# Attention scores of four heads in one four-bank tile, ordered behind earlier sums, in a fused attention and two-MLP kernel

## Chip, cores and metric

The kernel runs on one core of one Trainium2 chip. The metric is the device time of one execution in microseconds (us); smaller is better. Three runs of the kernel before took 642.29, 642.5 and 643.7 us.

## What is computed

```python
scores = (1/sqrt(64)) * q @ k.T            # 2 batches, 8 heads, 768 positions, 64 per head
keep = (pos < n_sink) | ((rel >= 0) & (rel < window))      # 4 sinks, window 128
a = softmax(where(keep, scores, -1e9))
x = (a @ v), heads side by side            # 1536 tokens x 512
h = x @ w_in                               # first MLP, 512 -> 2048 -> 512
x = (max(h, 0) + alpha * min(h, 0)) @ w_out
h = x @ w_in2                              # second MLP
out = max(h, 0)**2 @ w_out2
```

All of it is float32. The wide matmuls of the MLPs run as three products of a high and a low part (`PR`).

## The kernel before, in words

**Attention** (`Short.job`) is cut into 24 jobs: 12 chunks of 128 tokens (6 of each batch, in the order `ORDER`), each in two groups `g` of four heads. Four of the jobs (the first chunk of either batch) see one block of keys, the other 20 see the block before, the sinks and their own block. A job loads q and K (and v, for the first group), and then on TensorE (PE), VectorE (DVE), ScalarE (ACT) and GpSimd (POOL):

1. scores (PE, L522) of two heads at a time, `p` = 0 and 1, into the tile `s` of two banks; the two heads lie on partitions 0 to 63 and 64 to 127 of q and K. The single-block jobs put `p` = 1 into `ya0` and `ya1`;
2. per `p`: one predicated copy for the diagonal (DVE, L526), then per head a masked reduction that gives the scores and their minimum (DVE, L532, "the reductions" below) and an exponential with its sum (ACT, L536);
3. reciprocal and one scaling of all four heads (DVE, L541 to L548);
4. four transposes into `t` (PE, L556), and one of the sinks' part into `o` (PE, L562); copies of both to SBUF (`pc`, `ss`, on ACT or DVE);
5. two selects (POOL, L570) that part the two key blocks, `pp` and `pc`;
6. the sums a @ v (PE, L588) into `o`, and two copies, a high and a low part, into `X` (L249, L256).

**The MLPs** (`Feed`): the hidden dimension has 16 slices `f` of 128. `half` splits the loaded weights of one slice (input or output half) on DVE and ACT into a high and a low part: on DVE mostly a halving (L291, L293), a combination (L296) and the remainder (L256). `into` (PE, L315) makes h of one slice for a block of tokens in one bank, a unit, and ACT and DVE make `g` from it (L325 to L332). `outof` (PE, L347) adds a slice of g into the bank of output part `j`, and `finish` stores that bank. The first eight slices of the first MLP are done for three blocks of 512 tokens (`EARLY`) while the attention runs; for the first block `into` runs in two parts of 256 tokens, and the output parts `j` run in pairs, in the banks `ya0` and `ya1`. The rest follows when the attention is over (`late`).

**What sets the order.** The engines run fixed lists. `Plan.issue` makes them: each operation has a due time, a cost and what it needs, and the plan gives each engine the operation that can start first, ties by due time; operations with `SOON` go before all others. `JOBS`, `FIRST`, `EARLY_IN`, `EARLY_OUT` and `LOAD` are due times. An engine that waits for one instruction holds up all that stand behind it on its list. `WARM` matmuls of the identity (L696) stand at the start.

PSUM has eight banks: `h0`, `h1`, `ya0`, `ya1`, two of `s`, and one each of `t` and `o`.

Of the kernel before, what the change touches and what calls it, by code (L numbers as in the profile page):

```python
# [18 lines left out]
P = 128  # L19
NS = 32  # L20
# [13 lines left out]

NEAR = 25
# [8 lines left out]
EARLY_OUT = tuple(40 + 2 * f for f in range(8))  # L44
# [7 lines left out]
WARM = 10  # L52


class Plan:
# [4 lines left out]
    def __init__(self, start=()):  # L60
        self.ops, self.written, self.read, self.thin = [], {}, {}, set()
        self.free = dict.fromkeys(AFTER, 0.0)
        self.free.update(start)
# [19 lines left out]
    def until(self, start, cost, ticks, part):  # L83

        while True:
# [3 lines left out]
            ticks[k] = ticks.get(k, 0) + span * rate * part  # L89
# [5 lines left out]
    def issue(self):  # L95
        ops, free, ticks, turns = self.ops, self.free, {}, {}
# [11 lines left out]
        while could:  # L108
# [10 lines left out]
            free[e] = self.until(at, cost, ticks, 0.5 if i in self.thin else 1) if e == "pe" else at + cost  # L119
# [13 lines left out]


class Places:

    def __init__(self):
        self.specs = {}  # L140

    def put(self, pool, shape, dt, *keys):
        for k in keys:
            self.specs[k] = (pool, shape, dt)

    def new(self, key, shape=None, dt=None):
        made = []

        def get():
            if not made:  # L150
                pool, s, d = self.specs[key]
                made.append(pool.tile([P] + (shape or s), dt or d, tag=key, name=key))
            return made[0]
        return get
# [25 lines left out]
def attn_moe_moe(ctx, tc, q, k, v, vsink, par, alpha, w1, w2, out):  # L180
# [80 lines left out]
    class Feed:  # L261
# [3 lines left out]
        def __init__(self, plan, places, raws=lambda q: (q % 3, []), hs=("h0", "h1")):  # L265
            self.plan, self.places, self.raws, self.hs = plan, places, raws, hs
            self.halves = self.banks = 0
            self.w, self.g = {}, {}

        def half(self, due, layer, f, slot, a, need):  # L270
# [5 lines left out]
            r, more = self.raws(q)  # L276
            rk, ck, xk = f"raw{r}", f"cs{q % 2}", f"x{q % 2}"
# [5 lines left out]
            add(due - LOAD + a, more, [rk], ("dma", 1456, lambda: nc.sync.dma_start(out=raw(), in_=src)))  # L283
# [17 lines left out]
        def into(self, due, layer, f, slot, g, chunks, at=0):  # L301
# [3 lines left out]
            hk, rk = self.hs[self.banks % len(self.hs)], f"r{self.banks % 2}"  # L305
            self.banks += 1
# [3 lines left out]
            h, r, gt = new(hk), new(rk), self.g[g]  # L310
            for kt in range(KT):
                def mm(kt=kt):
# [5 lines left out]
                    (["late"] if hk[0] == "y" else []), [hk], ("pe", 3 * (n / 2.4 + 13.3), mm))  # L318
# [18 lines left out]
        def outof(self, due, layer, f, slot, g, j, bank, first, last):  # L337
# [65 lines left out]
    class Short:  # L403
# [3 lines left out]
        def __init__(self, plan, places, con, pool, psum):  # L407
# [7 lines left out]
            put(psum, [2, 512], F32, "s")  # L415
            put(psum, [4, P], F32, "t", "o")

        def add(self, *args):
            self.mine.append(self.plan.add(*args))
            return self.mine[-1]  # L420

        def masks(self):
# [33 lines left out]
            m = self.maskm  # L456
            nc.vector.tensor_scalar_mul(m[:, 0:NS], nosink[:, 0:NS], BIG)
            nc.vector.tensor_scalar_mul(m[:, NS:], outw, BIG)

            inw1 = mrel[:, 0:NS]  # L460
            nc.vector.tensor_scalar(inw1, rel[:, 0:NS], float(P), win_f, op0=ALU.add, op1=ALU.is_lt)
            nc.vector.tensor_tensor(out=inw1, in0=inw1, in1=nosink[:, 0:NS], op=ALU.max)
            nc.vector.tensor_scalar_mul(self.mask1[:, 0:NS], inw1, BIG)
            nc.vector.tensor_copy(out=self.mask1[:, NS:], in_=m[:, NS:])

        def start(self):
            self.K = [self.con.tile([P, 2, 4 * KC], F32, name=f"K{g}") for g in range(NG)]
            self.v, self.early = {}, self.places.new("g7")
# [11 lines left out]
        def job(self, i, b, c, g):  # L480
# [14 lines left out]
            self.load(due - 8, qk, qt, q[b, c, g].rearrange("p (a s) -> p a s", a=2), 364)  # L495
# [348 lines left out]
```

## Time and profile before

| | us |
|---|---|
| three runs: lowest, median, highest | 642.29, 642.5, 643.7 |
| the profiled execution: its own time | 642.0 |
| its span, first to last instruction | 640.3 |
| PE, DVE, ACT, POOL busy in the span | 623.1, 401.3, 240.8, 28.8 |
| first wide matmul (L315) | 29.43 |
| first `outof` matmul (L347) | 80.96 |
| PE's last matmul ends | 633.78 |

The profiled execution took 1.7 us more than its span. Busy time is a sum over instructions; PE's matmuls are pipelined and their ends are modelled, so a PE that is busy all the time can still lose time where it changes from one kind of matmul to another. That is read from the chain of work, where each piece begins where the one before it ends.

### The profile page before, as it was taken

Reading aid. Unit: us, or ns where it says so; the run is one execution under the profiler, and the core shown is the slowest. Engines: PE = TensorE matmul, PEld = TensorE weight load, DVE = VectorE, ACT = ScalarE, POOL = GpSimd, SP = SyncE. Lnnn points to the kernel's source line nnn. Section 1 sums busy time; section 2 is a strip of 40 time slices with the busy share of each in tenths; the row PEclk is TensorE's granted clock in tenths of the full one; section 3 lists DMA queues with packets and bytes.
Section 4 is the critical chain, followed back from the end, with each engine's and each line's share of the span. In section 5 each row is a group of like instructions: output and inputs, shape, how many; then the busy total and the mean of one; then the engine's idle time right before and its main releaser. Section 6 shows DMA issues by size and latency. Waiting matters only on the chain.

```text
span 640.3 us, 9043 instructions
## 1 busy us (share of the span) xinstructions
PE 623.1 (97%) x3400; PEld 511.1 (80%) x3400; DVE 401.3 (63%) x957; ACT 240.8 (38%) x551; POOL 28.8 (5%) x48
## 2 busy tenths in 40 slices
PE   5898999999999999999999999999999999999995
PEld 4697977777888888888888888888888888888884
DVE  7999976677885979445279993333396424344442
ACT  5888844344444725111035671111262211010110
POOL 0011212111200000000000000000000000000000
PEclk9889999999999999999999999999999999999998
DMA  8952322211063445000005540000030000101002
GB/s 277 369 199 71 106 69 66 79 39 34 1 203 127 137 157 167 33 1 0 1 1 167 195 137 29 0 1 0 1 132 1 1 0 1 66 1 42 25 0 72
DMA packets 23429, 48.14 MB, mean 75 GB/s; under 512 B 2512, under 2 KB 11984, under 8 KB 23376
## 3 DMA queue, kind: packets, MB, share of 16 engines
q1 hardware_dynamic: 23232, 47.34, 22.5%
q8 instruction: 29, 0.48, 0.3%
q14 instruction: 24, 0.20, 0.1%
q10 hardware_dynamic: 144, 0.13, 0.1%
HBM read 44.31 MB, written 3.15 MB: 74 GB/s over the span
## 4 chain that ended last, share of the span: by engine, by line
PE 92%; DVE 3%; DMA 3%; SPq 1%; issue 0%; ACT 0%; DVEq 0%; ACTq 0%
PE yb L347 31%; PE h L315 26%; PE ya L315 15%; PE ya L347 11%; PE o L588 4%; PE s L522 4%; PE t L556 1%; DMA Y<-w 1%; DMA K<-k 1%; DMA raw<-w 1%; DVE x L296 0%; DVE x L293 0%; DVE w L256 0%; PE o L562 0%; DVE sp L532 0%; SPq L283 0%
## 5 line engine op out<-in xcount | busy, mean ns | idle before, releaser
L315 PE MATMUL h<-X,w 128*128 128x512 f32 (+1 forms) x816 | 181.5, 371 | 1.1 <-DVE X L249 0.7
L315 PEld LDWEIGHTS h<-X,w 128*128 128x128 f32 x816 | 141.2, 190 | 28.3 <-DVE X L249 0.9
L347 PE MATMUL yb<-w,g 128*128 128x512 f32 x576 | 134.5, 389 | 0.0
L347 PEld LDWEIGHTS yb<-w,g 128*128 128x128 f32 x576 | 108.1, 188 | 22.4
L332 DVE TENSOR_TENSOR r<-r 128x512 f32<-128x512 f32 x48 | 33.1, 691 | 122.8 <-ACT r L330 122.8
L315 PE MATMUL ya<-X,w 128*128 128x512 f32 x432 | 103.9, 389 | 0.0
L315 PEld LDWEIGHTS ya<-X,w 128*128 128x128 f32 x432 | 81.1, 188 | 16.8
L347 PE MATMUL ya<-g,w 128*128 128x512 f32 x288 | 72.8, 400 | 0.0
L256 DVE TENSOR_TENSOR g<-r,g 128x512 fp32r<-128x512 f32 (+1 forms) x104 | 68.6, 659 | 2.5 <-ACT g L249 0.3
L347 PE MATMUL yb<-g,w 128*128 128x512 f32 x288 | 68.3, 390 | 0.0
L347 PEld LDWEIGHTS yb<-g,w 128*128 128x128 f32 x288 | 53.8, 188 | 12.1 <-DVE g L256 1.0
L347 PEld LDWEIGHTS ya<-g,w 128*128 128x128 f32 x288 | 52.1, 188 | 11.6 <-issue 0.2
L287 ACT ACTIVATE cs<-raw 128x512 f32<-128x512 f32 x56 | 37.1, 672 | 39.8 <-DVE x L296 25.5
L330 ACT ACTIVATE r<-ya 128x512 f32<-128x512 f32 x24 | 14.3, 597 | 96.3 <-PE ya L315 96.3
L536 ACT ACTIVATE sp<-sp,nm 128x160 f32<-128x160 f32 (+1 forms) x96 | 40.1, 419 | 26.8 <-DVE nm L532 26.5
L296 DVE SCALAR_TENSOR_TENSOR x<-cs,x 128x512 uint32<-128x512 uint32 x64 | 44.1, 694 | 2.1
L256 DVE TENSOR_TENSOR w<-x,w 128x512 fp32r<-128x512 f32 x64 | 43.9, 688 | 1.2
L330 ACT ACTIVATE r<-h 128x512 f32<-128x512 f32 x24 | 14.4, 598 | 78.2 <-PE h L315 78.2
L327 DVE SCALAR_TENSOR_TENSOR r<-r,oma,h 128x512 f32<-128x512 f32 (+1 forms) x44 | 28.3, 645 | 17.1 <-ACT r L325 16.9
L325 ACT ACTIVATE r<-h 128x512 f32<-128x512 f32 (+1 forms) x44 | 22.8, 517 | 34.1 <-PE h L315 33.8
L522 PE MATMUL s<-K,q 64*128 64x160 f32 (+1 forms) x320 | 32.1, 321 | 1.7 <-issue 1.5
L522 PEld LDWEIGHTS s<-K,q 64*128 64x128 f32 x320 | 24.4, 196 | 11.1 <-issue 8.2
(90 smaller groups left out, 536.8 us busy)
## 6 DMA issues: line engine op xcount, KB each, us to landing
raw<-w SPq DMA_DIRECT2D x56, 512.0 KB, 3.7
Y<-w SPq DMA_DIRECT2D x8, 512.0 KB, 7.0
K<-k SPq DMA_DIRECT2D x24, 160.0 KB, 3.0
v<-v SPq DMA_DIRECT2D x12, 256.0 KB, 2.7
out<-Y SPq DMA_DIRECT2D x11, 256.0 KB, 2.0
q<-q SPq DMA_DIRECT2D x20, 128.0 KB, 2.0
g<-q SPq DMA_DIRECT2D x4, 128.0 KB, 4.6
vs<-vsink SPq DMA_DIRECT2D x2, 256.0 KB, 5.8
```

What stands on the lines that cost most here:

```text
L256: nc.vector.tensor_tensor(out=lo, in0=src, in1=hi.bitcast(F32), op=ALU.subtract)
L287: add(at, [rk], [ck], ("act", 560, lambda: nc.scalar.activation(out=cs(), in_=raw()[:, :, 1].bitcast(F32), func=AF.Abs, scale=2.0 ** -112)))
L296: add(at, [ck, *two(xk)], two(xk), ("dve", dve_ns(512), lambda: nc.vector.scalar_tensor_tensor(out=x(), in0=cs().bitcast(U32), scalar=3, i ...
L315: nc.tensor.matmul(like(h()[:, 0:n], xs), lhsT=wi()[:, a, kt * P:(kt + 1) * P], rhs=xs, start=kt == 0 and i == 0, stop=kt == KT - 1 and i ...
L325: add(SOON + due, [hk], [rk], ("act", act_ns(n, True), lambda: nc.scalar.activation(out=rs(), in_=hs(), func=AF.Relu, scale=-1.0)))
L327: add(SOON + due, [hk, rk, "oma"], [rk], ("dve", dve_ns(n + 60), lambda: nc.vector.scalar_tensor_tensor(out=rs(), in0=rs(), scalar=oma[:, ...
L330: add(SOON + due, [hk], [rk], ("act", act_ns(n, True), lambda: nc.scalar.activation(out=rs(), in_=hs(), func=AF.Relu)))
L332: add(SOON + due, [rk], [rk], ("dve", dve_ns(n), lambda: nc.vector.tensor_tensor(out=rs(), in0=rs(), in1=rs(), op=ALU.mult)))
L347: nc.tensor.matmul(y(), lhsT=lhsT, rhs=rhs, start=first and i == 0, stop=last and i == 2)
L522: nc.tensor.matmul(bank(j)[:, x:y], lhsT=qt()[rows, p], rhs=K[rows, p, k0:k0 + y - x], start=True, stop=True)
L536: ("act", act_ns(n) + 186, lambda h=h: nc.scalar.activation(out=sp()[:, h, 0:n], in_=sp()[:, h, 0:n], func=AF.Exp, scale=-1.0, bias=nm()[: ...
L588: nc.tensor.matmul(po()[j * D:(j + 1) * D, p], lhsT=l, rhs=r, start=x == 0, stop=x == len(terms) - 1)
```

## The change

The scores of a job's four heads become one step, of 16 matmuls in the trace where two steps had 8 each, into one tile `s` of four banks. From the eleventh job on the step is told to follow the sums of the job two places ahead. The banks for that come from `ya0` and `ya1`: during the attention the units (`into`) and the first sums of the MLP (`outof`, now mostly one output part at a time) take turns in `h0` and `h1`. The predicated copy works on four heads. The scaling of step 3 may go to ACT as four instructions. The masks that the first jobs don't need become a planned step, 34 warm-up matmuls stand where 10 stood, due times and load times are new, and the plan counts a switch between kinds of PE work.

```diff
-JOBS = (0, 0.5, 1, 1.5, 12, 16, 20, 24) + tuple(range(40, 120, 5))
+JOBS = (0, 0.5, 1, 1.5, 10, 14, 18, 22) + tuple(range(38, 118, 5))
+JOB_LOADS = (-10, -10, -9, -8.5)
+VALUE_LOADS = {0: -8, 6: -6.5}
+RAW_LOADS = tuple(-9.5 + 1.5 * x for x in range(16))
+NFREE, BEHIND = 10, 2
-WARM = 10
+WARM = 34
...
-            put(psum, [2, 512], F32, "s")
+            put(psum, [4, 512], F32, "s")
...
-            for p in range(2):
-                if c == 0 and p:
-                    sk, both = ["ya0", "ya1"], [new("ya0"), new("ya1")]
-                    bank = lambda j, both=both: both[j]()
-                else:
-                    s, sk = new("s"), ["s"]
-                    bank = lambda j, s=s: s()[:, j]
...
+            s, at = new("s"), due
+            def scores():
+                for p in range(2):
                     for x, y, k0 in ((0, KC, before * KC), (KC, W3, here * KC)) if c else ((0, P, here * KC),):
                         for j in range(2):
                             rows = slice(j * D, (j + 1) * D)
-                            nc.tensor.matmul(bank(j)[:, x:y], lhsT=qt()[rows, p], rhs=K[rows, p, k0:k0 + y - x],
+                            nc.tensor.matmul(s()[:, 2 * p + j, x:y], lhsT=qt()[rows, p], rhs=K[rows, p, k0:k0 + y - x],
                                              start=True, stop=True)
...
+            add(SOON + at, [qk, ("K", g, here)] + ([("K", g, before)] if c else []), ["s"], ("pe", 930 if c else 420, scores),
+                after=self.sums[i - BEHIND] if i >= NFREE else ())
...
-                    add(at, sk, sk, ("dve", dve_ns(2 * P), lambda s=s: nc.vector.copy_predicated(
+                add(at, ["s"], ["s"], ("dve", dve_ns(4 * P), lambda: nc.vector.copy_predicated(
...
+            def each():
+                for h in range(4):
+                    nc.scalar.activation(out=sp()[:, h, win:n], in_=sp()[:, h, win:n], func=AF.Copy, scale=rc()[:, h:h + 1])
             add(due, [rck] + four(spk), four(spk), ("dve", dve_ns(4 * P), lambda: nc.vector.tensor_tensor(
-                out=sp()[:, :, win:n], in0=sp()[:, :, win:n], in1=rc().unsqueeze(2).to_broadcast([P, 4, P]), op=ALU.mult)))
+                out=sp()[:, :, win:n], in0=sp()[:, :, win:n], in1=rc().unsqueeze(2).to_broadcast([P, 4, P]), op=ALU.mult)),
+                ("act", 880, each))
...
-            for js in (range(0, 2), range(2, 4)):
+            for js in ((0, 1), (2,), (3,)) if i == 0 else ((0,), (1,), (2,), (3,)):
+                ys = [feed.bank() for _ in js]
```

How the lists move, at three places.

PE, in the middle of the attention (`ya` and the changed kernel's `h` are banks of output sums, `o<-ss`, `o<-pp`, `o<-pc` the six sums of a job, `s` scores, `t` transposes). Before:

```order
L588 MATMUL o<-pc_1444,v_1190 64x128 x2
L522 MATMUL s<-K_124,q_1401 128x160 x2
L522 MATMUL s<-K_124,q_1401 128x128 x2
L347 MATMUL ya_1194<-g_587,w_1_623 128x512 x3
L556 MATMUL t<-ident,sp_1432 128x128 x4
L562 MATMUL o<-ident,mask_97 128x128
L347 MATMUL ya_1203<-g_587,w_1_623 128x512 x3
L522 MATMUL s<-K_124,q_1401 128x160 x2
```

The first half of a job's scores stood behind sums, the second alone between wide matmuls. Now:

```order
L557 MATMUL t<-ident,sp_1414 128x128 x4
L563 MATMUL o<-ident,mask_94 128x128
L340 MATMUL h_1234<-g_856,w_1_1245 128x512 x3
L340 MATMUL h_1256<-g_856,w_1_1245 128x512 x3
L340 MATMUL h_1498<-g_479,w_1_802 128x512 x3
L340 MATMUL h_1498<-g_509,w_1_890 128x512 x3
L590 MATMUL o<-ss_1481,vs_452 64x128 x2
...
L590 MATMUL o<-pc_1479,v_1162 64x128 x2
L557 MATMUL t<-ident,sp_1468 128x128 x4
L515 MATMUL s<-K_115,q_1424 128x160 x2
L515 MATMUL s<-K_115,q_1424 128x128 x2
L515 MATMUL s<-K_115,q_1424 128x160 x2
L515 MATMUL s<-K_115,q_1424 128x128 x2
```

Both halves stand together behind the sums, here with the transposes of another job between; four groups of wide matmuls part a job's transposes from its sums.

DVE, at the first reductions of the program (`sp,nm<-s,mask`; `x` and `w` are weights being split). Before:

```order
L464 COPY mask_96<-maskm 128x128
L291 TENSOR_SCALAR x_145<-raw_127 128x512
L293 TENSOR_SCALAR x_145<-raw_127 128x512
L296 SCALAR_TENSOR_TENSOR x_145<-cs_143,x_145 128x512
L291 TENSOR_SCALAR x_161<-raw_137 128x512
L249 CAST w_0_164<-x_145 128x512
L293 TENSOR_SCALAR x_161<-raw_137 128x512
L256 TENSOR_TENSOR w_0_164<-x_145,w_0_164 128x512
L296 SCALAR_TENSOR_TENSOR x_161<-cs_159,x_161 128x512
L532 ISA sp_180,nm_181<-s,mask_97 128x128
```

Now:

```order
L462 COPY mask_93<-maskm 128x128
L528 ISA sp_150,nm_151<-s,mask_94 128x128
L528 ISA nm_151 128x1
L528 ISA sp_150,nm_151<-s,mask_94 128x128
L528 ISA nm_151 128x1
L528 ISA sp_150,nm_151<-s,mask_94 128x128
L528 ISA nm_151 128x1
L528 ISA sp_150,nm_151<-s,mask_94 128x128
L528 ISA nm_151 128x1
L284 TENSOR_SCALAR x_165<-raw_137 128x512
```

The first job's reductions moved ahead of the first weight work.

PE, from the last warm-up matmuls (`h<-ident`) to the first wide matmul of the changed kernel:

```order
L699 MATMUL h_330<-ident 128x128
L557 MATMUL t<-ident,sp_253 128x128 x4
L590 MATMUL o<-pc_300,v_211 64x128 x4
L557 MATMUL t<-ident,sp_296 128x128 x4
L590 MATMUL o<-pc_359,v_211 64x128 x4
L515 MATMUL s<-K_114,q_372 128x160 x2
L515 MATMUL s<-K_114,q_372 128x128 x2
L515 MATMUL s<-K_114,q_372 128x160 x2
L515 MATMUL s<-K_114,q_372 128x128 x2
L590 MATMUL o<-pc_382,v_211 64x128 x4
L308 MATMUL h_416<-X,w_0_214 128x256 x6
L308 MATMUL h_429<-X,w_0_290 128x256 x6
```

Four jobs' sums and five jobs' scores stand ahead of it; before, the first half of the sixth job's scores stood there too, and 10 warm-up matmuls instead of 34.

## Rows read from the trace of the kernel before

**Rows 1.** The page: busy time by engine, share of the span, instructions

```profile
PE 623.1 (97%) x3400; PEld 511.1 (80%) x3400; DVE 401.3 (63%) x957; ACT 240.8 (38%) x551; POOL 28.8 (5%) x48
```

**Rows 2.** Busy time by stretch: PE, PEld, DVE, ACT, POOL; granted clock; DMA share, GB/s

```profile
0.00:10.00 10.00, 5.93 (x30) 5.37 (x30) 7.25 (x31) 3.35 (x5) 1.14 (x8) 1.00 0.77 243
10.00:20.00 10.00, 7.13 (x42) 5.15 (x44) 8.79 (x44) 8.98 (x34) 0.00 (x0) 1.00 0.99 363
20.00:29.00 9.00, 7.21 (x54) 5.43 (x56) 9.00 (x33) 8.25 (x27) 0.00 (x0) 0.99 1.05 371
29.00:36.00 7.00, 6.89 (x41) 5.45 (x39) 6.97 (x24) 5.45 (x14) 1.41 (x2) 0.53 0.96 350
36.00:81.00 45.00, 43.22 (x432) 38.53 (x429) 44.81 (x146) 37.09 (x108) 7.68 (x10) 1.00 0.35 106
81.00:179.00 98.00, 98.00 (x812) 75.72 (x811) 68.20 (x235) 43.44 (x148) 18.62 (x28) 1.00 0.16 45
179.00:640.00 461.00, 454.74 (x2004) 375.44 (x2002) 256.31 (x455) 134.28 (x223) 0.00 (x0) 1.00 0.18 59
```

**Rows 3.** The chain of work in the middle of the attention: start us, us, what

```profile
99.68 1.46 PE o L588 x24
101.14 0.69 PE s L522 x8
101.83 0.90 PE ya L347 x3
102.73 0.44 PE t L556 x4
103.17 0.11 PE o L562
103.28 0.70 PE ya L347 x3
```

**Rows 4.** The chain of work, its first piece of L347

```profile
80.96 0.70 PE ya L347 x3
```

**Rows 5.** DVE's timeline at the last unit of the first block: start us, us

```profile
80.61 0.42 DVE L526 COPY_PREDICATED s<-tri,s 128x256 f32<-128x256 uint32 x1
80.94 0.68 DVE L548 TENSOR_TENSOR sp<-sp,rc 128x512 f32<-128x512 f32 x1
81.55 0.47 DVE L327 SCALAR_TENSOR_TENSOR r<-r,oma,h 128x256 f32<-128x256 f32 x1
```

**Rows 6.** Groups of DVE's instructions, 0 to 180 us: busy us, mean ns

```profile
L296 DVE SCALAR_TENSOR_TENSOR x<-cs,x 128x512 uint32<-128x512 uint32 x18 | 12.7, 712 | 0.1
L256 DVE TENSOR_TENSOR w<-x,w 128x512 fp32r<-128x512 f32 x16 | 11.0, 688 | 0.0
...
L293 DVE TENSOR_SCALAR x<-raw 128x512 uint16<-128x512 uint16 x10 | 4.3, 446 | 0.0
```

**Rows 7.** PE's timeline at the start

```profile
2.72 4.63 PE L696 MATMUL h<-ident 128*128 128x128 f32 x20 [2.72 <-POOL ident L439]
...
7.91 0.80 PE L522 MATMUL s<-K,g 64*128 64x128 f32 x4 [0.55 <-DMA K<-k]
...
29.43 1.01 PE L315 MATMUL h<-X,w 128*128 128x256 f32 x3
```

**Rows 8.** PE's waits in 0 to 70 us: total, times, longest

```profile
PE s L522 <- DVE nm L532: 2.0, 4, 0.8
```

**Rows 9.** The timeline of one job from its transposes to its sums

```profile
102.57 0.60 PE L556 MATMUL t<-ident,sp 128*128 128x128 f32 x4
...
103.27 0.69 DVE L249 COPY pc<-t 128x512 f32<-128x512 f32 x1 [0.31 <-PE o L562]
...
103.67 0.42 ACT L536 ACTIVATE sp<-sp,nm 128x160 f32<-128x160 f32 x1
...
104.73 0.64 POOL L570 TENSOR_SCALAR_AFFINE_SELECT pc<-pc 128x512 f32<-128x512 f32 x1
...
106.20 0.44 PE L588 MATMUL o<-ss,vs 128*64 128x128 f32 x4
```

More of the change, by code (lines that the diff above doesn't have):

```diff
@@ L51 @@
 NEND = 4
-WARM = 10
+WARM = 34
 class Plan:
     def __init__(self, start=()):
-        self.ops, self.written, self.read, self.thin = [], {}, {}, set()
+        self.ops, self.written, self.read, self.kind = [], {}, {}, {}
         self.free = dict.fromkeys(AFTER, 0.0)
@@ L81, in add, with until @@
         return i
-    def until(self, start, cost, ticks, part):
+    def until(self, start, cost, ticks):
         while True:
@@ L88, in until @@
             span = min((k + 1) * TICK - start, cost / rate)
-            ticks[k] = ticks.get(k, 0) + span * rate * part
+            ticks[k] = ticks.get(k, 0) + span * rate
             cost -= span * rate
@@ L95, in issue @@
     def issue(self):
[L96 removed]
+        ops, free, ticks, turns, kind = self.ops, self.free, {}, {}, None
         then, left, ready = [[] for _ in ops], [len(o[1]) for o in ops], [[0.0] * len(o[2]) for o in ops]
@@ L118, in issue @@
             _, cost, run = ops[i][2][x]
-            free[e] = self.until(at, cost, ticks, 0.5 if i in self.thin else 1) if e == "pe" else at + cost
+            if e == "pe":
+                kind, last = self.kind.get(i), kind
+                free[e] = self.until(at, cost + (SWITCH if kind != last else 0), ticks)
+            else:
+                free[e] = at + cost
             if ops[i][3]:
@@ L276, in half @@
             r, more = self.raws(q)
+            early = RAW_LOADS[q:q + 1] if self.early else ()
             rk, ck, xk = f"raw{r}", f"cs{q % 2}", f"x{q % 2}"
@@ L282, in half @@
             at = due - PARTS + a
-            add(due - LOAD + a, more, [rk], ("dma", 1456, lambda: nc.sync.dma_start(out=raw(), in_=src)))
+            add(early[0] if early else due - LOAD + a, more, [rk], ("dma", 1456, lambda: nc.sync.dma_start(out=raw(), in_=src)))
             half = lambda dt, j: x().bitcast(dt).rearrange("p (j w) -> p j w", w=2)[:, :, j]
@@ new lines, in job @@
+            self.plan.kind[self.mine[-1]] = "scores"
+            if c:
+                add(at, ["s"], ["s"], ("dve", dve_ns(4 * P), lambda: nc.vector.copy_predicated(
+                    out=s()[:, :, W3 - P:W3], mask=self.tri.unsqueeze(1).to_broadcast([P, 4, P]), data=s()[:, :, 0:P])))
+            for h in range(4):
+                at = due + .4 * h
+                add(at, ["s", "masks" if c else "mask0"], [(spk, h), (nmk, h)], ("dve", dve_ns(n) + 8, lambda h=h:
+                    nc.vector.tensor_tensor_reduce(
+                        out=sp()[:, h, 0:n], in0=s()[:, h, lo:lo + n], in1=mask, scale=-SCALE, scalar=3e38,
+                        op0=ALU.add, op1=ALU.min, accum_out=nm()[:, h:h + 1])))
+                add(at + 1, [(spk, h), (nmk, h)], [(spk, h), (smk, h)],
+                    ("act", act_ns(n) + 190, lambda h=h: nc.scalar.activation(
+                        out=sp()[:, h, 0:n], in_=sp()[:, h, 0:n], func=AF.Exp, scale=-1.0,
+                        bias=nm()[:, h:h + 1], accum_out=sm()[:, h:h + 1])))
@@ L588, in mm @@
                             nc.tensor.matmul(po()[j * D:(j + 1) * D, p], lhsT=l, rhs=r, start=x == 0, stop=x == len(terms) - 1)
-                add(SOON + due + 2, [x for _, need in terms for x in need], ["o"], ("pe", 205 * len(terms) + 100, mm))
+                self.sums[i].append(add(SOON + due + 2, [x for _, need in terms for x in need], ["o"],
+                                        ("pe", 205 * len(terms), mm)))
+                self.plan.kind[self.sums[i][-1]] = "sums"
             xs = [X[:, e, 2 * g:2 * g + 2, ci * P:(ci + 1) * P] for e in range(2)]
```

107 lines of the change are left out of this document (43 added, 64 removed).

## The prediction

> **What bounds the kernel now.** I read the busy times first: PE is busy 623.1 of 640.3 us [rows 1]. By stretch [rows 2] the reader should see three regimes. From 81 us to the end PE never stops (98.00 of 98.00, then 454.74 of 461 with the last stores behind it), so there only fewer or cheaper PE steps gain anything. From 20 to 81 us DVE is full (9.00 of 9, 6.97 of 7, 44.81 of 45) and PE is full too but for 0.11 us and 1.78 us; whichever gets more work loses. Before 20 us neither is full: DVE idles 2.75 + 1.21 = 3.96 us, PE 6.9 us. From 29 to 36 us the granted clock is 0.53, that is, nearly all at 1.2 of 2.4 GHz, after PE had idled 1.79 of the 9 us before. Busy PE hides what a step really takes, so prices come from the chain of work [rows 3].
>
> I cut the program at the first matmul of L347, 80.96 us [rows 4], which needs nearly the same work done in both kernels, and price the two sides apart.
>
> **Behind the cut: PE's price.**
>
> *Merged scores.* A step of scores takes 0.69 us in the chain, and the three wide matmuls behind it 0.90 instead of 0.70, 0.20 more [rows 3]. So a step alone among wide matmuls costs 0.89 us. Put behind the other half it saves the way in and out. Its eight matmuls then cost between 0.69 (no gain inside the step) and little more than the streams; the nearest row is the sums, 24 small matmuls without a change of kind in 1.46 us, 0.061 each, 0.49 for eight. I take 0.49: saving 0.40 a job, bounds 0.20 (only the 0.20 behind it) and 0.45. By the lists twelve jobs' scores stand behind the cut: 12 × 0.40 = **4.8** (2.4 to 5.4).
>
> *A page against it.* In the trace the eight weight loads of a step fit, with all else, in 0.69 us. The Trainium skill ("TensorE: Matmul & The Clock Gate", "LDWEIGHTS" and Part 3) gives columns/1.2, so 107 ns for 128 columns, and says that a load overlaps running matmuls only where its row group differs; one after another eight loads would be 0.85 us, the merge would save 0.04 a job, and the sum would lose 12 × 0.36 = 4.3 us, an estimate from that page. The trace speaks against that reading: 0.69 is less than 0.85, so the two row groups' loads run beside each other.
>
> *What is owed at the cut.* By the lists, before still owes 25 half steps of scores, 14 sets of transposes and 14 of the sinks' transposes there; the changed kernel owes 24, 13 and 13; the sums are 14 in both. That is 0.89 + 0.44 + 0.11 = **1.4** less [rows 3]; its other side is in the front.
>
> *Transposes between sums and scores.* Four times behind the cut the list has sums, transposes, scores: one change of kind more each. Bounds 0 and 0.20 (what wide matmuls paid behind scores); I take 0.20, as it lies nearest: **−0.8**.
>
> *New stalls.* The last operations before a job's sums run in series: transposes at 102.57, a copy, two selects that end at 104.73 + 0.64 = 105.37, sums at 106.20 [rows 9]: 2.80 needed, 0.83 spare. In the changed list the same stretch holds the transposes, the sinks' transposes and four groups of wide matmuls, 0.44 + 0.11 + 4 × 0.70 = 3.35 [rows 3]: 0.55 spare. And the copy stands on ACT in 20 of 24 jobs (16 before), where an exponential takes 0.42 [rows 9]. A copy one exponential late just fits, two are 0.29 late. Bounds 0 and 0.29 × 14 = 4.1; I take 0.05 a job, as most copies should find the queue that the plan expects: **−0.7**.
>
> *Single output parts in `h0`, `h1`.* A part's bank is wanted again two groups later, 24 wide matmuls or 8 × 0.70 = 5.6 us on; the copy to SBUF is hidden under that. In the first block parts 0 and 1 end together and part 2 waits for part 0's copy as it did in `ya0`: nothing. If the cover went, each would cost about one copy, 0.69 us [rows 9], three to five times.
>
> **Ahead of the cut: DVE's price.** DVE's last operation that belongs ahead of the cut is the reading of the first block's last unit, at 81.55 us [rows 5]. Counted in the lists up to it, the changed kernel has 5 scalings fewer at 0.61 each (80.94 to 81.55 [rows 5]; they go to ACT as four instructions each), 15 predicated copies of 256 at 0.33 (80.61 to 80.94) against 8 of 512 at up to twice that (I take 0.60), one weight combination and one remainder fewer and three halvings fewer (0.71, 0.69 and 0.45 [rows 6], each less the 0.07 to 0.10 by which neighbours overlap: 0.62, 0.60, 0.36), but 3 copies of the transposes more (0.69 [rows 9], so 0.60): 3.05 + 0.15 + 1.22 + 1.08 − 1.80 = 3.7 us less DVE work. ACT has the room: 37.09 of 45 us, and the scalings that moved are three in the first 40 us.
>
> DVE's idle 3.96 us can shrink, since q and K are loaded ahead of the first weights (before, the first scores waited for K until 7.91 us) [rows 7] and the reductions come first; it can also grow, because the weight splitting that filled those gaps now stands behind them. Its bounds: 3.96 gained, or, with the low clock below, some 5.7 lost. I take 1 us lost, near no change, since both reasons hold. So the front is **+2.7**, bounds −2 and +7.6.
>
> What PE would allow there is more: clock 0.47 × 7 = 3.3 us, idle 1.9, eight merged steps 3.2, and an earlier first wide matmul. DVE's list ahead of the last remainder of the fourth job's X is shorter by two combinations, three remainders, three scalings and a few reductions less three copies, over 4 us, so the first wide matmul should come at about 25 instead of 29.43 [rows 7]. PE will then wait for split weights: what it gains there beyond DVE's 2.7 is lost again in waits.
>
> *Warm-up.* 10 instructions (20 matmuls) took 4.63 us [rows 7], so 24 more are up to 11 us at 1.2 GHz, half at 2.4. PE idles 4.07 + 2.87 + 1.79 = 8.7 us in the first 29 [rows 2]. At the higher clock they hide; if the clock stays low they delay the first jobs by 11 − 8.7 = 2.3 us and more where idle time falls in the wrong place: that is the low end of the front.
>
> *Loads.* K of the fifth job stands behind eight weight loads and all early q, K and v on SP's queue, one of those loads waiting for DVE and ACT to free its buffer: 6.0 MB at 363 GB/s [rows 2] is 17 us, about 19 us with the start, before its scores are due: nothing. If it slipped, scores and all of PE's list would wait.
>
> **Sum.** 4.8 + 1.4 − 0.8 − 0.7 + 2.7 = 7.4 us. The profiled execution took 642.0 (span 640.3 and 1.7 around it): 634.6. The median of the runs, 642.5, is 0.5 above it; from there it is 635.1, and I predict **635.0 us**.
>
> **Rivals.**
>
> *A. The one tile stalls every job (slower).* With two half steps, scores of `p` = 1 waited for the reductions of `p` = 0. Now the scores of a job need all four reductions of the job before, and behind the waiting scores stand all wide matmuls. For it: while DVE is full its list runs late, and PE waited four times for that, 2.0 us, 0.8 the longest [rows 8]. Against it: the job before had its scores one set of sums earlier, 106.20 − 99.68 = 6.5 us [rows 3, 9], and DVE has 30 of 98 us free behind the cut. At 0.8 us in each of 20 jobs, 16 us: 635 + 16 = 651. It decides once the waits pass 7.4 / 20 = 0.37 us a job. Chance 0.08.
>
> *B. The front opens.* DVE's idle goes instead of growing, the clock rises early and stays. The front gives 7.6 instead of 2.7: 630. The clock row speaks for it: the clock fell after idle time that 24 more matmuls fill. The Trainium skill ("TensorE: Matmul & The Clock Gate", "HAM oscillation") says likewise that waits between bursts of matmuls let the clock fall back. Against it is DVE's full list. Chance 0.22.
>
> *C. The front loses.* Warm-up matmuls at the low clock and new gaps on DVE: −2 instead of +2.7, 639.7. Chance 0.15.
>
> *D. The merge saves only the change behind it,* because the second half costs a full 0.69: 0.20 a job, 2.4 instead of 4.8: 637.4. What the Trainium skill's page on TensorE says of loads, above, leans this way. Chance 0.08.
>
> *E. Transposes to sums too tight:* 4.1 instead of 0.7: 638.4. Chance 0.07.
>
> **How the numbers follow.** My forecast, 632 to 638, has 0.40. The range 628 to 641 holds it with B, C, D and E but for their tails, and leaves out A. A change under 0.2%, 1.3 us, can't be told from none here. Slower: A and a tenth of C and E together, 0.09. Same: 0.04. Faster: 0.87.
>
> **What would show it.** In the chain behind the cut: scores as one piece of 16 of about 1.2 us behind sums (0.69 + 0.49; more than 1.35 means D), PE without idle time, the first L340 matmul at 77 to 79 us. At 74 B holds, at 82 C. Waits of scores for the reductions of more than 7 us in total mean A; waits of sums for POOL of over 3 us mean E. The first wide matmul should come at about 25 us with the clock at 1.00 behind it. I am wrong if the gain lies mostly ahead of the cut, or if PE is idle for some us between the cut and the attention's end.

## The result, and the profile after

The changed kernel took 633.98 us, median of four runs (632.97 to 635.78); the kernel before, on the same chip, 642.61 (642.29 to 643.7). The ratio is 0.9866, 95% interval 0.984 to 0.9892: 8.6 us faster. The forecast was 635.0, range 628 to 641, so the time, its sign and the likeliest case held. Not all of the steps did.

The profiled execution of the changed kernel is the slowest of its four: 635.78 us, span 634.1. Against the profiled one of before (642.0, 640.3) the gain is 6.2 us, and this is the number to hold against the sum of 7.4. Of the other three the time and the mean granted clock are on record: 634.45 us at 0.996, 633.5 and 632.97 at 0.999; the profiled one has 0.994.

Busy time on the page, to be read against [rows 1]:

```profile
PE 618.5 (98%) x3448; PEld 512.4 (81%) x3448; DVE 390.3 (62%) x927; ACT 248.5 (39%) x579; POOL 29.1 (5%) x48
```

Busy time by stretch, columns as in [rows 2]; the cut at 81 us is the same, behind it the attention now ends near 172 us:

```profile
0.00:10.00 10.00, 7.28 (x41) 6.56 (x42) 5.42 (x31) 3.96 (x12) 1.14 (x8) 1.00 0.71 199
10.00:20.00 10.00, 9.51 (x79) 8.29 (x80) 8.58 (x38) 7.74 (x31) 0.00 (x0) 1.00 0.98 357
20.00:29.00 9.00, 7.59 (x52) 5.85 (x51) 7.39 (x20) 6.53 (x17) 0.00 (x0) 0.62 0.91 312
29.00:36.00 7.00, 6.72 (x62) 6.26 (x61) 7.00 (x25) 6.74 (x22) 0.00 (x0) 1.00 0.80 264
36.00:81.00 45.00, 40.90 (x427) 36.42 (x425) 45.00 (x147) 40.70 (x121) 10.38 (x13) 1.00 0.48 144
81.00:172.00 91.00, 90.44 (x791) 72.84 (x790) 66.55 (x235) 47.94 (x160) 17.59 (x28) 1.00 0.21 61
```

From 81 us to the end of the attention PE still hardly stops. Ahead of it DVE is full from 29 to 81 us and PE no longer is: 4.1 us idle from 36 to 81 where it had 1.78. In the first 29 us DVE works 5.42 + 8.58 + 7.39 = 21.39 us; before it was 7.25 + 8.79 + 9.00 = 25.04 [rows 2]. So its idle time there grew by 3.65 us.

The chain of work in the middle of the attention, in order of time (start, us, what), against [rows 3]:

```profile
105.22 0.59 PE t L557 x4
105.80 1.19 PE s L515 x16
106.99 0.26 PE o L563
107.25 1.40 PE h L340 x6
...
110.11 1.19 PE s L515 x16
111.30 0.90 PE h L340 x3
112.20 0.44 PE t L557 x4
```

The scores of four heads are one piece of 1.19 us between sums and wide matmuls. The three wide matmuls behind it still pay the way out, 0.90 us. A job's scores used to cost 2 × (0.69 + 0.20) = 1.78; they now cost 1.19 + 0.20 = 1.39.

PE's timeline at its first wide matmul and at its first matmul of L340 (L347 before), the cut, against [rows 4, 7]:

```profile
27.80 2.43 PE L308 MATMUL h<-X,w 128*128 128x256 f32 x14
...
79.76 0.71 PE L340 MATMUL h<-g,w 128*128 128x512 f32 x2
```

PE's waits from 78 to 180 us, all that there are:

```profile
PE o L563 <- DVE mask L542: 0.4, 1, 0.4
```

From the cut to the start of PE's last matmul it was 552.6 us (80.80 to 633.38) and is 548.1 (79.76 to 627.86). So 4.5 us came from behind the cut, where 4.7 were forecast, and 1.0 from ahead of it, where 2.7 were. The other 0.7 lie behind the start of PE's last matmul, where none were: the span ended 6.9 us after it and now ends 6.2 after it, as in every other run below (6.15 to 6.35). (The cut of before is 80.96 in the chain and 80.80 in the record of the matmul itself; I use the record from here on.)

Busy time from the start to the cut, first before, then now:

```profile
0.00:80.80 80.80, 70.18 (x586) 59.74 (x587) 76.62 (x268) 63.06 (x181) 10.22 (x20) 0.96 0.61 205
0.00:79.76 79.76, 70.75 (x648) 62.36 (x648) 72.16 (x253) 64.42 (x195) 11.26 (x20) 0.96 0.64 204
```

DVE has 4.46 us less work there (72.16 against 76.62) and 3.42 us more idle time (7.60 against 4.18). The difference is the 1.0 us.

### The profile page after: what moved, and what is told of

Read it like the earlier page. It is cut to its first block, busy times and chain, and to the rows that moved or that the text cites. A ratio compares the mean times of both kernels' runs of the same rounds, so it can differ in the third digit from the quotient of the medians.

```text
span 634.1 us, 9086 instructions
## 1 busy us (share of the span) xinstructions
PE 618.5 (98%) x3448; PEld 512.4 (81%) x3448; DVE 390.3 (62%) x927; ACT 248.5 (39%) x579; POOL 29.1 (5%) x48
## 4 chain that ended last, share of the span: by engine, by line
PE 80%; DVE 13%; DMA 3%; issue 1%; SPq 1%; ACT 1%; DVEq 0%; ACTq 0%
PE h L308 35%; PE yb L340 28%; PE h L340 10%; PE o L590 4%; PE s L515 3%; DVE w L247 2%; DVE x L289 2%; DMA al<-alpha 2%; DVE r L320 1%; DVE x L286 1%; PE t L557 1%; DVE g L247 1%; DVE sp L528 1%; DMA raw<-w 1%; DVE X L247 1%
## 5 line engine op out<-in xcount | busy, mean ns | idle before, releaser
L308 PE MATMUL h<-X,w 128*128 128x512 f32 (+1 forms) x1248 | 275.9, 375 | 0.3 <-DVE r L320 0.3
L308 PEld LDWEIGHTS h<-X,w 128*128 128x128 f32 x1248 | 222.3, 189 | 42.8 <-DVE r L320 0.7
L340 PE MATMUL yb<-w,g 128*128 128x512 f32 x576 | 134.5, 389 | 0.0
L340 PEld LDWEIGHTS yb<-w,g 128*128 128x128 f32 x576 | 108.1, 188 | 22.4
L323 ACT ACTIVATE r<-h 128x512 f32<-128x512 f32 x48 | 28.7, 598 | 174.5 <-PE h L308 174.4
L340 PE MATMUL h<-g,w 128*128 128x512 f32 x288 | 69.5, 395 | 0.1
L340 PE MATMUL yb<-g,w 128*128 128x512 f32 x288 | 68.7, 391 | 0.2 <-DVE g L247 0.2
L340 PEld LDWEIGHTS yb<-g,w 128*128 128x128 f32 x288 | 53.7, 188 | 12.7 <-DVE g L247 1.6
L340 PEld LDWEIGHTS h<-g,w 128*128 128x128 f32 x288 | 53.2, 189 | 11.4 <-ACT Y L240 0.6
L320 DVE SCALAR_TENSOR_TENSOR r<-r,oma,h 128x512 f32<-128x512 f32 (+1 forms) x56 | 37.2, 666 | 36.3 <-ACT r L318 36.3
L240 DVE CAST g<-r 128x512 fp32r<-128x512 f32 (+1 forms) x69 | 29.1, 422 | 2.8
L240 DVE CAST w<-x 128x512 fp32r<-128x512 f32 x25 | 10.6, 425 | 28.8 <-PE h L308 18.6
L240 ACT CAST w<-x 128x512 fp32r<-128x512 f32 x39 | 24.0, 616 | 7.1 <-DVE x L289 6.4
L286 DVE TENSOR_SCALAR x<-raw 128x512 uint16<-128x512 uint16 x56 | 25.5, 460 | 1.0 <-DMA raw<-w 0.8
```

The source lines that it names most:

```text
L240: return lambda: f(**dict(zip(("out", "in_"), get())))
L286: add(at, [rk], [(xk, 0)], ("dve", dve_ns(512, True), lambda: nc.vector.tensor_scalar(half(U16, 0), raw().bitcast(U16).rearrange("p j (w a ...
L308: nc.tensor.matmul(like(h()[:, 0:n], xs), lhsT=wi()[:, a, kt * P:(kt + 1) * P], rhs=xs, start=kt == 0 and i == 0, stop=kt == KT - 1 and i ...
L320: add(SOON + due, [hk, rk, "oma"], [rk], ("dve", dve_ns(n + 60), lambda: nc.vector.scalar_tensor_tensor(out=rs(), in0=rs(), scalar=oma[:, ...
L340: nc.tensor.matmul(y(), lhsT=lhsT, rhs=rhs, start=first and i == 0, stop=last and i == 2)
```

## Experiments

Each edit is to the changed kernel unless it says otherwise. "Behind the cut" is the time from the first matmul of L340 to the start of PE's last one, in the profiled execution. The kernel before took 641.7 to 642.1 us beside these runs.

| run | median us | ratio to before, 95% interval | cut us | behind the cut us |
|---|---|---|---|---|
| before | 642.61 | 1 | 80.80 | 552.6 |
| changed kernel | 633.98 | 0.9866 (0.984 to 0.9892) | 79.76 | 548.1 |
| a2_again | 633.83 | 0.9871 (0.9855 to 0.9886) | 80.01 | 547.5 |
| x1_foreign | 642.26 | 1.0013 (1.0002 to 1.0023) | 79.36 | 554.9 |
| x2_same | 637.18 | 0.9925 (0.9912 to 0.9938) | 79.00 | 551.0 |
| x3_nobehind | 635.2 | 0.9899 (0.9884 to 0.9913) | 78.33 | 548.5 |
| x4_warm10 | 636.97 | 0.9923 (0.9903 to 0.9942) | 81.06 | 547.4 |
| x5_front | 652.01 | 1.0145 (1.0129 to 1.0162) | 94.43 | 551.6 |
| x6_noact | 634.58 | 0.9885 (0.987 to 0.99) | 78.28 | 548.2 |
| x7_warm60 | 636.68 | 0.9923 (0.9909 to 0.9936) | 80.94 | 547.4 |
| x8_dve | 645.19 | 1.0044 (1.003 to 1.0058) | 88.77 | 548.1 |
| x9_pool | 642.76 | 1.0008 (0.9999 to 1.0017) | 94.02 | 540.7 |
| x10_oldtimes | 633.16 | 0.9867 (0.9851 to 0.9882) | 74.18 | 551.0 |
| x12_old34 | 633.02 | 0.9862 (0.9846 to 0.9879) | 73.69 | 551.4 |

The last two columns can be compared where the lists owe the same attention at the cut. Against the changed kernel x9 owes two jobs' scores and sums fewer, x10 and x12 one job more, x3, x6 and x7 one job's transposes more (0.55 us by the chain), and the kernel before half a step of scores and one job's transposes more (the 1.4 us of the forecast).

**The merge: part the two halves again.** x1 puts one identity matmul between the halves of each of the 20 two-block jobs, x2 two more score matmuls of the same kind; the second half of the scores writes over both.

```diff
 for p in range(2):
+    if c and p:      # x1
+        nc.tensor.matmul(s()[:, 3, 0:P], lhsT=self.ident, rhs=self.ident, start=True, stop=True)
...
+    if c and p:      # x2
+        for j in range(2):
+            rows = slice(j * D, (j + 1) * D)
+            nc.tensor.matmul(s()[:, 2 + j, 0:P], lhsT=qt()[rows, p],
+                             rhs=K[rows, p, here * KC:here * KC + P], start=True, stop=True)
```

> The changed kernel with one identity matmul of another kind (128 rows instead of 64, 128 columns) put between the two halves of the scores of each of the 20 two-block jobs; its result is overwritten, the lists are otherwise the same. Theory 1 (the gain behind the first outof is the way in and out of a kind of matmul that the merge saves, about 0.4 us a job): each of the 20 costs one way out and in plus its own two passes, some 0.3 to 0.4 us; the 12 behind the first outof count in full, those ahead are partly hidden by DVE: 4 to 7 us more than the changed kernel's 634.0, so 638 to 641, and more than the variant with two more matmuls of the same kind. The piece of scores in the chain grows from 1.19 us to 1.5 or more. Rival (the gain comes from less DVE work and the new loads, a change of kind costs no more than its stream): 20 times 0.11 at most, about 1.5 us, 635.5, and less than the same-kind variant.

> The changed kernel with two more matmuls of 128 columns of the same kind (64 rows, both row halves) between the two halves of each two-block job's scores; their result is overwritten. Both theories: only their streams, four passes in two pairs, 0.1 to 0.25 us a job, 12 behind the first outof in full: 1.5 to 3.5 us more than 634.0, so 635.5 to 637.5. Theory 1 says that this is less than the variant with one foreign matmul, the rival that it is more.

The chain of work of x1, in the same place:

```profile
106.04 0.59 PE t L559 x4
106.62 0.69 PE s L517 x8
107.32 0.42 PE s L512 x2
107.73 0.69 PE s L517 x8
```

And that of x2:

```profile
104.64 0.59 PE t L562 x4
105.22 0.69 PE s L520 x8
105.92 0.22 PE s L514 x4
106.14 0.49 PE s L520 x8
```

In x2 the second half is a piece of its own, 0.49 us: the estimate that was taken from the sums' 0.061 a matmul. In x1, behind a foreign matmul, it is 0.69 again, and the foreign matmul takes 0.42 where the two of the same kind take 0.22. x1 holds less work than x2 and is 5.1 us slower. So it is the change of kind that costs. Twelve jobs behind the cut at 0.20 + 0.42 = 0.62 are 7.4 us; behind the cut x1 lost 554.9 − 548.1 = 6.8. One needless matmul a job takes away all that the change gives. The eight jobs ahead of the cut pay the same price, 5.0 us in all, and the cut did not come later (79.36 against 79.76). But 79.76 is from the changed kernel's slowest execution. By the medians x1 lost 8.3 us, 1.5 more than behind the cut: PE has room ahead of it for most of the 5.0 us, not for all.

**The place behind the sums.** x3 takes away the rule that the scores follow the sums of the job two places ahead; the merged tile stays.

```diff
-NFREE, BEHIND = 10, 2
+NFREE, BEHIND = 99, 2
```

> The changed kernel without the rule that puts scores behind the sums of the job two places ahead (each job's scores are still one step of four heads). Changes of kind on PE's list from the first wide matmul on: 73 instead of 66 (94 in the kernel before). Theory 1 (0.2 us for each change): 7 more, 1.4 us, about 635.4. Rival (placement is what counts, merging the halves is not): most of the gain behind the first outof goes, 4 us or more, 638 or more.

It took 635.2 us, about 1.2 more than the changed kernel, which is just what can't be told from nothing here. Behind the cut it is 548.5 against 548.1, with 0.55 us more owed. PE's list has 73 changes of kind from the first wide matmul on (transposes counted with the wide matmuls), against 66 with the rule and 94 in the kernel before. The seven lie behind the cut, and the 0.2 us that was expected for each does not show there. The tile merges the halves; the rule adds little.

**DVE sets the front.** x8 doubles the early weights' remainders (the second result is the same as the first and written over it), which adds 16 operations of some 0.6 us to DVE.

```diff
+low = lo_op(lambda: (w()[:, 1], x().bitcast(F32), w()[:, 0]), 512)
+if early:
+    low = (("dve", low[0][1], lambda go=low[0][2]: (go(), go())),)
-add(at + 2, [*two(xk), (wk, 0)], [(wk, 1)], *lo_op(lambda: (w()[:, 1], x().bitcast(F32), w()[:, 0]), 512))
+add(at + 2, [*two(xk), (wk, 0)], [(wk, 1)], *low)
```

> The changed kernel with each of the 16 early weight remainders done twice on DVE (0.6 us each, 9.6 us in all, the same result; the plan does not know of it, so all lists are otherwise the same). Theory 1 (DVE bounds the front): the first outof comes 6 to 10 us later than at 79 us and the total rises by as much, 640 to 644. Rival (chains of waits or PE bound it): 3 us or less, 637 or less.

The cut came at 88.77 instead of 79.76, 9.0 us later for 9.6 us of work, and behind it nothing changed (548.1); by the medians it lost 11.2. With x1 this is the pair that was wanted: of 5.0 us more work on PE ahead of the cut some 1.5 reach the time, of 9.6 on DVE nearly all or all.

**Can work be taken from DVE?** x6 lets no scaling go to ACT; x9 lets the early remainders go to GpSimd (`low` is that of x8, undoubled; 14 of 16 went).

```diff
-    in1=rc().unsqueeze(2).to_broadcast([P, 4, P]), op=ALU.mult)),
-    ("act", 880, each))
+    in1=rc().unsqueeze(2).to_broadcast([P, 4, P]), op=ALU.mult)))      # x6
...
+if early:                                                              # x9
+    low += (("pool", 1200, lambda: nc.gpsimd.tensor_tensor(
+        out=w()[:, 1], in0=x().bitcast(F32), in1=w()[:, 0].bitcast(F32), op=ALU.subtract)),)
```

> The changed kernel with all 24 scalings on DVE, as before (the changed kernel has 6 on ACT, 5 of them ahead of the first outof). Changes of kind 68 instead of 66. Theory 1 (DVE's full list bounds the front): 5 times 0.61 = 3 us more DVE work ahead of the first outof, 1.5 to 4 us more than 634.0. Rival (ACT's chains bound it as much, or PE): within 1 us of 634.0.

> The changed kernel with the plan free to put the 16 early weight remainders on GpSimd (14 of them go there: 8.4 us of DVE work less ahead of the first outof). Theory 1: DVE is eased, the front gains until PE or the chains bind, 2 to 5 us less than 634.0, 629 to 632, if GpSimd takes not much more than the 1.2 us that the plan assumes. Rival (chains bind, or GpSimd's longer operations delay the selects and the splitting): 634 or more.

Both missed. x6 took 634.58 us, and its cut, 78.28, is not later. Its stretch from 36 to 81 us:

```profile
36.00:81.00 45.00, 42.92 (x433) 37.88 (x432) 45.00 (x142) 35.07 (x102) 9.25 (x12) 1.00 0.42 128
```

DVE is full there as in the changed kernel, and ACT has 35.07 us of work instead of 40.70. Up to its cut DVE has 10 scalings instead of 6, some 2.5 us more, but two halvings and two casts to `g` fewer, and its busy time there is 72.70 us against 72.16. The plan puts other operations that have a choice in the place of the scalings, so which engine a scaling goes to decides little.

x9 took 642.76 us, no better than the kernel before. Groups of its first 90 us, by shape (busy us, mean ns, idle time before):

```profile
L294 POOL TENSOR_TENSOR w<-x,w 128x512 fp32r<-128x512 f32 x14 | 18.8, 1350 | 36.2 <-ACT w L240 34.7 <-DVE w L240 1.4
L289 DVE SCALAR_TENSOR_TENSOR x<-cs,x 128x512 uint32<-128x512 uint32 x18 | 14.0, 787 | 0.0
L247 DVE TENSOR_TENSOR g<-r,g 128x256 fp32r<-128x256 f32 x14 | 8.8, 630 | 0.0
```

The same two groups on DVE in the changed kernel, and the remainders that are on DVE there:

```profile
L289 DVE SCALAR_TENSOR_TENSOR x<-cs,x 128x512 uint32<-128x512 uint32 x18 | 12.5, 696 | 0.0
L247 DVE TENSOR_TENSOR w<-x,w 128x512 fp32r<-128x512 f32 x16 | 10.9, 682 | 0.0
L247 DVE TENSOR_TENSOR g<-r,g 128x256 fp32r<-128x256 f32 x16 | 7.3, 459 | 0.0
```

GpSimd needs 1350 ns for what DVE does in 682, and some of DVE's own operations stretch: 459 to 630 ns and 696 to 787 in the mean. They are few: of the 14 subtractions for `g` four took 847 to 1499 ns, the other ten 406 to 418, and three of the four ran while GpSimd subtracted. So a remainder that is worth 0.6 us on DVE gives part of that back. The plan also filled DVE's list again: up to the cut it has 12 casts to `g` instead of 6 and 7 copies of the sinks' part instead of 1, and ACT 4 and 1 instead of 9 and 6; two jobs' scores and sums more stand ahead of the cut here, which explains part of these counts. PE's waits ahead of the cut are for DVE's scalings (5.3 us), `X` (3.5) and masks (1.5), none of them for weights from GpSimd. How much of the 8.8 us each of these takes wasn't parted.

**The new times alone, and the change without them.** x5 is the kernel before with the new due times, load times and 34 warm-up matmuls; x10 is the changed kernel with all times and the 10 warm-up matmuls of before. The edit of x10:

```diff
-JOBS = (0, 0.5, 1, 1.5, 10, 14, 18, 22) + tuple(range(38, 118, 5))
+JOBS = (0, 0.5, 1, 1.5, 12, 16, 20, 24) + tuple(range(40, 120, 5))
-EARLY_OUT = tuple(44 + 2 * f for f in range(8))
+EARLY_OUT = tuple(40 + 2 * f for f in range(8))
-WARM = 34
+WARM = 10
...
-when = JOB_LOADS[i] if i < 4 else due - 8
+when = due - 8
```

> The kernel before with the changed kernel's due times, load times and 34 warm-up matmuls, but with scores in half steps, the banks ya0 and ya1, the copy per half and all scalings on DVE as before. Changes of kind on PE's list from the first wide matmul on: 100 (94 before, 66 in the changed kernel). Theory 1 (behind the first outof only the merge gains, ahead of it only what DVE is spared): the clock is up early, but DVE's list is as long as before: 0 to 2 us less than before from the earlier start, 1 us more for 6 changes, so 640 to 643. Rival (the loads and the warm-up open the front by themselves): 3 us or more less than before, 639 or less.

> The changed kernel with all times of the kernel before (jobs' due times, first sums' due times, load times, 10 warm-up matmuls); the scores' one tile, the banks, the plan's switches and the place behind the sums stay. Theory: behind the cut nothing changes, 547.5 to 549.5 us from the first L340 matmul to PE's last; the front loses what early loads and warm-up give (scores wait for K until 7.9 us again, and the run with 10 warm-up matmuls lost 3 us): first L340 at 80.5 to 84, total 636.5 to 640. Rival (the new times give nothing, as the run with the times alone was slower than the kernel before): within 1 us of the changed kernel or faster, first L340 at 79 or earlier. If the front's new times and the merge only work together, the total is above 641.

> The changed kernel once more, unaltered, so that its neighbours in this batch have it on their own chip. Theory: 633 to 635 us, 7 to 9 below the kernel before. Its profile shows which of the two sides of the cut (the first matmul of L340 that sums the MLP) varies between executions: I expect 548 to 548.5 us from the cut to PE's last matmul again, and all variation, up to 1.5 us, ahead of it (78.3 to 80).

x5 missed both expectations: 652.01 us, 10 slower than the kernel before. Its cut came at 94.43; its stretch from 36 to 81 us:

```profile
36.00:81.00 45.00, 38.22 (x322) 32.23 (x322) 43.13 (x133) 34.85 (x97) 7.42 (x10) 0.85 0.44 141
```

PE is idle for 6.8 us there and DVE for 1.9, at a clock of 0.85. Why the old banks and the new times fit so badly was not taken further. But x5's lists owe the same at the cut as the changed kernel's (24 half steps of scores, 13 sets of transposes, 14 of sums), so the two can be compared behind it: 551.6 against 548.1 and 547.5. That is 3.5 to 4.1 us for the merge, with its transposes and stalls, where the steps made 4.8 − 0.8 − 0.7 = 3.3.

x10 missed the theory too, and here the rival held: 633.16 us, against 633.83 for the changed kernel on the same chip. **The new times give nothing; all of the gain is in the tile, the banks and the plan that goes with them.** The first 29 us of x10 in one stretch, and then the changed kernel's:

```profile
0.00:29.00 29.00, 17.28 (x124) 13.38 (x124) 24.43 (x100) 21.14 (x68) 1.14 (x8) 0.82 0.87 291
```

```profile
0.00:29.00 29.00, 24.37 (x169) 20.70 (x170) 21.40 (x88) 18.23 (x58) 1.14 (x8) 0.88 0.87 288
```

DVE, which sets the front, does 24.43 us of work there with the old times and 21.40 with the new. DVE's waits in the same 29 us say why; of the changed kernel, and then of x10:

```profile
DVE sp L528 <- PE s L515: 1.3, 2, 1.1
DVE parf L443 <- DMA pari<-par: 1.3, 1, 1.3
DVE pp L437 <- POOL pc L430: 1.2, 1, 1.2
DVE x L286 <- DMA raw<-w: 0.8, 1, 0.8
DVE rc L537 <- ACT sp L532: 0.7, 1, 0.7
DVE x L284 <- DMA raw<-w: 0.6, 1, 0.6
DVE oma L695 <- DMA al<-alpha: 0.5, 1, 0.5
DVE s L522 <- PE s L515: 0.4, 1, 0.4
DVE X L240 <- PE o L590: 0.4, 1, 0.4
```

```profile
DVE parf L443 <- DMA pari<-par: 1.3, 1, 1.3
DVE pp L437 <- POOL pc L430: 1.2, 1, 1.2
DVE rc L537 <- ACT sp L532: 0.6, 2, 0.3
DVE x L284 <- DMA raw<-w: 0.5, 1, 0.5
DVE sp L528 <- PE s L515: 0.3, 1, 0.3
DVE x L284 <- DMA Y<-w: 0.3, 1, 0.3
```

The rows add up to 7.2 and 4.2 us, so they hold the whole difference of 3.0. DVE waits for PE 2.1 us instead of 0.3 (scores, the first sums) and for loads, `par` aside, 1.9 instead of 0.8: the reductions stand ahead of the splitting that used to fill such gaps, and q and K are loaded ahead of the weights. PE's scores start earlier, 5.58 instead of 7.98 us, and PE is not what the front waits for. Part of the 3.0 us belongs to the one execution: x3 runs the changed kernel's lists on PE, DVE, ACT and GpSimd until 60 us, and there DVE works 22.82 us in the first 29. At the cut x10 owes one job more than the changed kernel: scores 1.39, two sets of transposes 0.88, the sinks' 0.11 and sums 1.46, together 3.8 by the chain; 551.0 is 2.9 more than 548.1 and 3.5 more than 547.5.

The changed kernel once more (a2) took 633.83 us with 547.5 behind the cut, 0.5 less than the lower end expected. Again the profiled execution, 635.61, was the slowest of its four.

**Warm-up and clock.** The changed kernel with 10 and with 60 warm-up matmuls, and x10 with 34:

```diff
-WARM = 34
+WARM = 10      # x4_warm10; 60 in x7_warm60
```

> The changed kernel with 10 warm-up matmuls as before instead of 34. Theory 1 (the front is bound by DVE's list and the chains of the first jobs; the warm-up raises the clock in the first 22 us, and shortens those chains): 0.5 to 2 us more than 634.0. Rival (PE's clock in the front decides): 3 us or more, 637 or more, with the granted clock at half until about 29 us or later. If the warm-up only fills idle time: no change.

> 60 warm-up matmuls instead of 34. Theory (DVE's list sets the front; the clock costs something only where PE has no room left): the clock stays high until the first wide matmul, first L340 matmul at 78 to 79 us, total within 1 us of the changed kernel on the same chip. Rival 1 (the low clock still costs the changed kernel its front): 1.5 us or more faster, first L340 at 77 or earlier. Rival 2 (warm-up matmuls stand in the way of the first jobs' scores and sums): 1.5 us or more slower, first L340 at 80.5 or later.

> The kernel with the times of before (x10_oldtimes), now with 34 warm-up matmuls instead of 10. There the granted clock was 0.55 from 10 to 20 us while PE was busy 5.75 of 10 us. Theory (PE has room in the front, DVE's list sets it): the clock is 1.00 from 10 us on, and the total stays within 1 us of x10_oldtimes, 632.5 to 634.5. Rival 1 (the low clock costs the front): 630 to 632. Rival 2 (warm-up matmuls delay the first jobs, as 60 did with the new times): 635 or more. If it comes out at 636 to 637 like 10 and 60 with the new times, the number of warm-up matmuls acts by the order the plan makes of it, not by the clock.

With the new times both edits lose: 636.97 is 3.0 us above 633.98, and 636.68 is 2.9 above 633.83, on the same chip. With the old times 10 and 34 are the same, 633.16 and 633.02. Stretches of the start, of x7, x10 and x12 in this order (the column before the last two is the granted clock):

```profile
10.00:20.00 10.00, 10.00 (x85) 8.93 (x84) 9.38 (x44) 8.74 (x34) 0.00 (x0) 1.00 0.99 374
```

```profile
10.00:20.00 10.00, 5.75 (x36) 4.12 (x36) 8.27 (x38) 8.87 (x35) 0.00 (x0) 0.55 0.98 347
```

```profile
10.00:20.00 10.00, 9.01 (x80) 7.63 (x80) 8.52 (x48) 8.90 (x36) 0.00 (x0) 1.00 1.00 361
```

x10 runs this stretch at 0.55 and x12 at 1.00, for the same time. x7 runs at 1.00 all through and is slow: PE is busy 10.00 of 10 and then 9.00 of 9, and the first wide matmul comes at 30.28 instead of 27.80, behind the warm-up. So with the old times the clock of the first 30 us decides nothing.

With the new times it does count. The 36 matmuls from the fourth job's transposes to the first wide matmul, in the changed kernel's profile and in x3's, which has the same lists there:

```profile
22.20:27.80 5.60, 5.41 (x36) 4.14 (x37) 4.46 (x10) 3.94 (x8) 0.00 (x0) 0.50 0.83 276
21.90:25.50 3.60, 3.15 (x36) 2.38 (x36) 3.45 (x9) 2.91 (x8) 0.00 (x0) 1.00 0.94 330
```

At a granted clock of 0.50 they take 5.60 us and at 1.00 3.60. The first wide matmul comes at 27.80 and at 25.54, and DVE's list runs 1.7 us behind x3's from 30 to 50 us and 0.75 from 55 to 65. The eight executions of the changed kernel on record also go by their mean clock: four at 0.998 and 0.999 took 632.97 to 633.69 us, four at 0.994 and 0.996 took 633.97 to 635.78. PE's waits just before, from 19 to 23 us, add up to 1.7 us in the changed kernel's profile and 1.8 in x3's, so why the clock fell in the one and not in the other stays open. x4's 3 us stay open too: the clock was low there as in x10 (0.72 from 10 to 20 us), and its list also differs.

x10 and x12 are the lowest times measured, 0.7 to 1.0 us below the changed kernel, which is under what can be told apart.

## Why the prediction was right, and where it was not

**Held.** *The merged scores*: 0.39 a job against 0.40, shown from both sides by x1 and x2. The second half costs 0.49 and not a full 0.69, so rival D is out. The Trainium skill's rule on weight loads ("TensorE: Matmul & The Clock Gate", "LDWEIGHTS"), read as loads one after another, would have left 0.04 a job, an estimate from that page; the trace, with 0.49 for eight, disagrees with that reading. *New stalls*: the one wait behind the cut is 0.4 us, against 0.7; no wait of scores for reductions (rival A), and sums waited for POOL once in the first 90 us, for 0.6 us (rival E). *Transposes between sums and scores*: 0.59 instead of 0.44, 0.15 each against 0.20. *Behind the cut* 4.5 and 5.1 us in two profiles, against 4.7. *DVE as the price of the front*: x8 and x1.

**Failed: the front's idle time on DVE.** "I take 1 us lost, near no change, since both reasons hold." It was 3.65 us in the first 29 us of the profile and 3.42 up to the cut. The term was inside its bounds (3.96 gained, 5.7 lost) and mis-sized; the other term, 3.7 us less DVE work, came out at 4.46. Together they leave 1.0 of the +2.7, and the cut came at 79.76 and 80.01, not at 77 to 79. The fall of the clock is part of it: the changed kernel's two profiles have the first wide matmul at 27.80 and 28.10 instead of about 25, and x3, without that fall, has it at 25.54. But x3's DVE too idles 2.2 us more than before in the first 29, so 1 us was too little in any case.

**Failed: the scalings that go to ACT.** They carried 3.05 of the 3.7 us. x6, without them, is 0.6 us above the changed kernel, which can't be told from nothing, and its DVE works 72.70 us up to the cut against 72.16. So the size of DVE's list was counted nearly right, and its cause was not: an operation taken off a full engine's list gives a gain only while the plan does not put others in its place.

**Failed: load times and warm-up as a gain.** The step said that idle time "can shrink, since q and K are loaded ahead of the first weights". x10 shows that without these times the kernel is as fast. Rival B, that the front opens by 7.6 us when the clock rises early, is out: x7 has the clock at 1.00 throughout and its cut at 80.94, and x12 gains nothing on x10. What a fall of the clock costs is smaller, 1.7 us of DVE's list at most. The 1.2 GHz at which the prediction puts the first warm-up matmuls stands in no row; [rows 2] has a granted clock of 1.00 there.

**A reading.** The prediction calls PE full from 20 us on but for 0.11 and 1.78 us; [rows 2] has 1.79 us of idle time from 20 to 29 as well. It uses that number elsewhere, and no term of the sum rests on it.

**Why the sum was right nevertheless.** In profiles the sum was 7.4 and the gain 6.2, 6.4 with a2: the front gave 1.7 less than forecast, the part behind the cut 0.2 less, and the end 0.7 that no step had. The medians gained 8.6, since the other executions of the changed kernel took 632.97 to 634.45. That the median came within 1.0 us of 635.0 is therefore in part luck. Where those executions found 1.3 to 2.8 us was not profiled. Behind the cut the two profiles agree to 0.6 us, and the others had the higher clock, which fell ahead of the cut in the profiles, so it is likelier to be there. For x10 and x12 an estimate by the chain's prices: at the debt of the changed kernel their cuts would come at 74.18 + 3.8 = 78.0 and, with one more of the sinks' transposes owed, 73.69 + 3.9 = 77.6, against 80.80 + 1.4 = 82.2 for the kernel before. That is 4.2 and 4.6 us, where the forecast in these terms was 2.7 + 1.4 = 4.1, and it came without the new times. Which of the bank scheme, the merged copies and the plan's switches gives it stays open.

## What to carry to other kernels

Small matmuls pay for their neighbours: here a step of eight costs 0.69 us behind another kind and 0.49 behind its own, 0.20 more falls on the wide matmuls behind, and one foreign matmul in between costs 0.6. Count changes of kind on the busy engine's list before counting instructions, and test the price, as the seven changes of x3 did not show it. And find out which engine sets each stretch before improving it: ahead of the cut early loads and warm-up helped PE, which had room for most of it, and left DVE, which had none, idle for longer.

## What the runs showed of the hardware that was not expected

A single 128-column identity matmul between two halves of scores cost more (0.42 us, and 0.20 on the half behind it) than two score matmuls (four in the trace, 0.22 us). GpSimd's 128x512 subtraction took 1350 ns against 682 on DVE, and DVE's 128x256 subtractions grew from 459 to 630 ns in the mean in the kernel that had it, by four of 14 that took 847 to 1499. A granted clock of 0.55 over 10 us, with PE busy for 5.75 of them, went with no change of the median (633.16, and 633.02 at 1.00); in the kernel with the new times the same 36 matmuls took 5.60 us at 0.50 and 3.60 at 1.00, and executions with the lower mean clock were the longer ones.
